# Mamba-2 scan followed by a hardswish MLP: row sums by token through transfers and squares of 32, narrower idle products, decoding steps and the parts of the first weights in another order

## The chip, the cores and the metric

The kernel runs on one core of one Trainium2 chip. The time is the device time in microseconds (us) of one launch; 337.93 us is the median of three runs of the kernel before (337.47 to 337.95). A profile of one more execution goes with it. Engines are named as the profile names them: PE (TensorE, matmuls), PEld (its weight loads, which run beside the matmuls), DVE (VectorE), ACT (ScalarE), POOL (GpSimd) and SP (SyncE, which here only issues transfers; SPq is its queue).

## The reference, cut to what matters

Two blocks follow each other. The first is a state-space scan with batch 4, 8 heads, 768 tokens, head size 32 and state size 16; the second is an MLP over 3072 tokens with 256 inputs, 2048 hidden units and 256 outputs. The MLP weights arrive as 64-bit floating point.

```python
log_a = np.log(np.clip(a, 1e-06, 1.0))
...
cum = np.cumsum(la, axis=-1)                          # within a chunk
L = np.exp(cum[:, :, :, None] - cum[:, :, None, :]) * causal
M = np.einsum('bhin,bhjn->bhij', Cc, Bc) * L
y[:, :, sl] = M @ xc + np.einsum('bhin,bhnd->bhid', Cc, state) * np.exp(cum)[..., None]
state = np.exp(np.sum(la, axis=-1)) * state + (B x, faded to the end of the chunk)
...
h = x @ w_in
g = h * np.clip(h + 3.0, 0.0, 6.0) / 6.0
out = g @ w_out
```

(The einsums are shortened; the results are the same.)

## The kernel before, in words

The 768 tokens are cut into 6 chunks of 128, for all 4 batches and 8 heads at once, so that a chunk has 32 (batch, head) pairs and the MLP sees 512 tokens of it. Each chunk c goes through the scan (decay squares `L`, products of C and B called `cb`, own products with `x` and products with the carried state) and then through the MLP as stage k = c: sixteen tiles f of 128 hidden units, each an accumulation of two fp32 products 128x512 into one of four PSUM banks (`f0` to `f3`), then ACT's `ramp` (L793) and DVE's `times_ramp` (L798), which frees the bank for tile f + 4. The second weight product follows as `first_out` (L811) in stage 0 and in other forms in the later stages. From stage 1 on, the first product is made of three products of rounded parts (hi, lo and less, L754). The scan of chunk k + 1 is written out by hand between the instructions of stage k: every engine has one queue, which it works off in program order, and the kernel says in program order what stands in it.

What the change and the prediction touch:

- **Decoding** (`decode`, L185 to L244). The weights are loaded as raw 32-bit words in eight parts (four of `w_in`, four of `w_out`) and turned into fp32 by steps that `weights(i, n)` advances: ACT copies the top words (L202); DVE masks exponent and sign (L221, L223) and starts the significand (L207); ACT makes the scale in two steps (L227, L229); DVE ends the significand (L211), joins exponent and sign (L234) and multiplies (L244). Three raw buffers are shared by the parts; `load_w(i + 3)` (L144) is issued in the step of L229 and waits until L211 of part i has read its buffer. In stage 0 the list `weave` puts step j of part i behind tile f = 4i - 8 + j; the fifth step of part i stands behind tile f = 4i - 4.
- **Row sums** (`add_up`, L289: a DVE scan). `cum` holds the running sums of log a for 32 rows (pairs) by 768 tokens. Chunks 2 to 5 need them also by token, as a bias for each partition: `turn_cum` transposes four squares 32x128 on PE into PSUM (L336, `c_ps`, bank `f1`), and `by_token` has DVE negate them into `cum_n` (L339). ACT's `decay` (L420) reads `cum_n` as the bias of its exponentials.
- **Rows from DRAM.** `store_rows` (L306, L308) writes `cum` to DRAM, `load_eto` (L328) and `load_decay` (L321) read it back spread over partitions; POOL's `conceal` (L162) masks `L` before ACT's `decay`.
- **Idle products** (`busy`, L528). Two fp32 products 128x512 of the identity with itself, whose result is not used, stand in PE's queue ahead of `scores(0)` (L565), which waits for `cT`, made by DVE (`turn_squares` L500, `part_heads` L510).
- **Parts of w_in** (`in_parts`, L723 on ACT, L726 and L729 on DVE) and of y (`split_y`, L743 on ACT, L744 and L746 on DVE). They live in buffers that earlier tensors leave: the hi part of part 2 in that of `w_in[1]` (tag `w1`), that of part 3 in `w2`, `y_hi` in `w0`.
- **First product of stage 0** (`mlp_in`, L686). Its last 16 products of 32 are cut in halves of 256 columns.

Of the kernel before, what the change touches and what calls it, by code (L numbers as in the profile page):

```python
# [8 lines left out]
FP32 = mybir.dt.float32  # L9
# [3 lines left out]
F32R = mybir.dt.float32r  # L13
# [8 lines left out]
def kernel(  # L22
# [167 lines left out]
    def decode(i):  # L190

        n = NK * FP * P
        top = raws[i].bitcast(U16).rearrange("p (n w) -> p n w", w=4)[:, :, 3]
        lo, hi = (raws[i].rearrange("p (n w) -> p n w", w=2)[:, :, w] for w in range(2))
        s = att.tile([P, n], U16, name="ws")
        e = att.tile([P, n], U16, name="we")
        m = att.tile([P, n], U32, name="wm")  # L200
        for sl in (slice(0, n),) if i != 1 else (slice(0, n // 2), slice(n // 2, n)):
            nc.scalar.copy(out=s[:, sl], in_=top[:, sl])  # L202
            if i == 1 and sl.start == 0:
                yield

        def significand():
            nc.vector.tensor_scalar(  # L207
                out=m, in0=hi, scalar1=0xFFFFF, scalar2=0x100000,
                op0=ALU.bitwise_and, op1=ALU.bitwise_or)
            yield  # L210
            nc.vector.scalar_tensor_tensor(  # L211
                out=m.bitcast(FP32), in0=lo, scalar=2.0 ** -32, in1=m, op0=ALU.mult,
                op1=ALU.add)
            yield

        parts_m = significand()
        if i == 0:
            next(parts_m)
            next(parts_m)
        yield  # L220
        nc.vector.tensor_scalar(  # L221
            out=e, in0=s, scalar1=0x7FF0, scalar2=None, op0=ALU.bitwise_and)
        nc.vector.tensor_scalar(  # L223
            out=s, in0=s, scalar1=0x8000, scalar2=None, op0=ALU.bitwise_and)
        next(parts_m, None)
        yield
        nc.scalar.activation(e.bitcast(BF16), e, AF.Relu, bias=bias_hi, scale=-8.0)  # L227
        yield
        nc.scalar.activation(e, e.bitcast(BF16), AF.Relu, bias=bias_lo, scale=-1.0)  # L229
        next(parts_m, None)  # L230
        if i and i + NRAW < 2 * NP:
            load_w(i + NRAW)
        yield
        nc.vector.tensor_tensor(out=e, in0=e, in1=s, op=ALU.bitwise_or)  # L234
        if i == 0:
            yield
        m, e = m.bitcast(FP32), e.bitcast(BF16)
        if i < NP:
            dst = w_in[i]
            m, e = (t.rearrange("p (k f) -> p k f", k=NK) for t in (m, e))  # L240
        else:
            dst = w_out[:, (i - NP) * FP:(i - NP + 1) * FP, :]
            m, e = (t.rearrange("p (k f) -> p k f", k=FP) for t in (m, e))
        nc.vector.scalar_tensor_tensor(  # L244
            out=dst, in0=m, scalar=2.0 ** -20, in1=e, op0=ALU.mult, op1=ALU.mult)
# [85 lines left out]

    cum_n = const.tile([P, NC, G], FP32, name="cum_n")

    def turn_cum(c_ps):
        for c in range(2, NC):
            nc.tensor.transpose(out=c_ps[:, c], in_=cum_c[:, c], identity=ident[:G, :G])  # L336

    def by_token(c_ps):
        nc.vector.tensor_scalar(  # L339
            out=cum_n[:, 2:], in0=c_ps[:, 2:], scalar1=-1.0, scalar2=None, op0=ALU.mult)  # L340


    yTs, states, mids, bTs, bss, tmps = {}, {}, {}, {}, {}, {}
# [181 lines left out]
    def busy(n, bank):  # L525

        for _ in range(n):
            nc.tensor.matmul(  # L528
                out=bank.rearrange("p (b i) -> p b i", b=NB), lhsT=ident,
                rhs=ident.unsqueeze(1).to_broadcast([P, NB, P]), start=True, stop=True)  # L530

    def from_state(c, a, pairs=range(NQ)):

# [144 lines left out]

    gTs, outs = {}, {}

    def mlp_in(k, f):
        h = ps.tile([P, TB], FP32, name="h", tag=f"f{f % 4}")
        for j in range(NK):
            n = TB // (1 + (f * NK + j >= NF * NK - 16))
            for t in range(0, TB, n):
                nc.tensor.matmul(  # L686
                    out=h[:, t:t + n], lhsT=w_in[f // FP][:, j, f % FP * P:(f % FP + 1) * P],
                    rhs=yTs[k][:, j].rearrange("p b i -> p (b i)")[:, t:t + n],
                    start=(j == 0 and t == 0), stop=True, skip_group_check=True)
        ramp(k, f, h)  # L690
        times_ramp(k, f, h)

    NJ = NF // 2
    EPS = 2.0 ** -12
# [2 lines left out]
    def in_parts(i):  # L702

        n = FP * P  # L710

        def one(pool, tag):
            t = pool.tile([P, NK, n], F32R, name="w_part", tag=tag)
            return [t[:, j] for j in range(NK)]

        def two(tag):
            return [att.tile([P, n], F32R, name="w_part", tag=tag) for _ in range(NK)]

        hi = one(const, f"w{i - 1}" if i > 1 else f"hi{i}")
        lo = one(const, f"lo{i}") if i < 2 else one(att, "wm") if i == 2 else two("ws")  # L720
        less = one(const, f"less{i}") if i < 2 else one(att, "wm") if i == 2 else two("we")
        for j in range(NK):
            nc.scalar.activation(hi[j], w_in[i][:, j], AF.Copy, scale=(1.0 - EPS / 2) * EPS)  # L723
        for j in range(NK):
            yield
            nc.vector.scalar_tensor_tensor(  # L726
                out=lo[j], in0=hi[j].bitcast(FP32), scalar=-1.0 / EPS, in1=w_in[i][:, j],
                op0=ALU.mult, op1=ALU.add)
            nc.vector.tensor_tensor(  # L729
                out=less[j], in0=lo[j].bitcast(FP32), in1=hi[j].bitcast(FP32), op=ALU.subtract)  # L730
        w_parts[i] = (hi, lo, less)
        yield

    def split_y(k):
        hi = const.tile([P, NK, TB], F32R, name="y_hi", tag="w0")
        lo = att.tile([P, NK, TB], F32R, name="y_lo", bufs=1)
        less = att.tile([P, NK, TB], F32R, name="y_less", bufs=1)
        for a in range(2):
            for u in range(2):
                y = yTs[k][:, u, :, HALF[a]] if k == 1 else ys[k][a, u]  # L740
                h, l = (t[:, u].rearrange("p (b i) -> p b i", b=NB)[:, :, HALF[a]]
                        for t in (hi, lo))
                nc.scalar.activation(h, y, AF.Copy, scale=1.0 - EPS / 2)  # L743
                nc.vector.tensor_tensor(out=l, in0=y, in1=h.bitcast(FP32), op=ALU.subtract)  # L744
        for j in range(NK):
            nc.vector.scalar_tensor_tensor(  # L746
                out=less[:, j], in0=lo[:, j].bitcast(FP32), scalar=-1.0 / EPS,
                in1=hi[:, j].bitcast(FP32), op0=ALU.mult, op1=ALU.add)
        y_parts[k] = (hi, lo, less)
# [41 lines left out]
    def ramp(k, f, h):  # L791

        nc.scalar.activation(  # L793
            gTs[k][:, f], h, AF.Relu, bias=half, scale=1.0 / 6.0)
# [85 lines left out]
    def split_quarter(k):  # L880
# [3 lines left out]

        halves = [g_quarter(k, 1, 1)[:, j * NJ // 2:(j + 1) * NJ // 2] for j in range(2)]
        hi, lo, less = quarter_parts[k] = [], [], []
        homes = ((ffn, "wide"), (ffn, "back")), ((const, "w0"), (att, "y_lo"))
        for where, g in zip(homes, halves):
            h, l = (home(*w) for w in where)
            hi.append(h)  # L890
# [213 lines left out]
            sums(c)  # L1104
        mix(c)

    def results(c):
        if c == 1:
            keep(c)
        split_y(c)  # L1110
        if TURN <= c < NC - 1:
            take(c)
        if TURN < c < NC - 1:
            renew(c)
# [69 lines left out]
    for k in range(NC):  # L1184
        gTs[k] = ffn.tile([P, NF, TB], FP32, name="gT")
        c, ahead = k + 1, k + 2
        if k == 0:
            for f in range(NF):
                mlp_in(k, f)
                for i in weave.get(f, []):  # L1190
                    weights(i, 1)
                if f in (6, 8):
                    diff_exp(c, f // 2 - 3)
            weights(NP + 1, 1)
            add_up(ends_at[1])
            store_rows()
            load_eto(c)
            rows(ahead)
# [6 lines left out]
            for i in range(NP):  # L1205
                for b in range(NB):
# [3 lines left out]
                    if (i, b) == (1, 0):  # L1210
                        renew(0)
                    if (i, b) == (1, 1):
                        c_ps = ps.tile([P, NC, G], FP32, name="c_ps", tag="f1")
                        turn_cum(c_ps)
                        by_token(c_ps)
                    if (i, b) == (2, 0):
                        conceal(ahead, 0)
                        conceal(ahead, 1)
# [4 lines left out]
                    elif (i, b) == (1, 3):  # L1223
# [1 line left out]
                        wake(c)  # L1225
                        turn(c, 0)
                        load_bc(ahead)
                        for n in (0, 0, 1):
                            next(ins[n])
                    elif (i, b) == (2, 3):  # L1230
                        decay(ahead, 0)
# [5 lines left out]
                        next(ins[1])  # L1237
                    elif (i, b) == (3, 1):
                        own_products(c)
                        results(c)  # L1240
                        next(ins[2])
                        decay(ahead, 2)
                    elif (i, b) == (3, 2):
                        rows(ahead + 1)
                        decay(ahead, 3)
                        from_start(ahead)
                    elif (i, b) == (3, 3):
                        for q in range(NB):
                            ends(ahead, q)
            lead_on(c)  # L1250
            next(ins[2])
            next(ins[2])
            continue
        if c == NC:
# [129 lines left out]
```

## Time and profile before

| what | value |
|---|---|
| median of 3 runs | 337.93 us (337.47 to 337.95) |
| the profiled execution, its time | 337.99 us |
| its span, first to last instruction | 336.2 us |
| PE busy | 329.7 us (98%) |
| DVE / ACT / POOL busy | 265.4 (79%) / 207.8 (62%) / 130.3 us (39%) |
| stage 0, first product (L686) | 21.4 to 49.0 us |
| stage 0, second product (L811) and scan of chunk 1 | 49.0 to 84.4 us |

How to read it: a group's line gives the code line, engine, operation, output <- inputs, shapes and count, then busy time and mean duration, then the idle time of the engine just before it and what ended that. A timeline line gives the start and the length of a run of equal instructions, and in brackets the idle time before it with its releaser. Consecutive instructions of one engine overlap in these rows, because a row ends when the result is written; so two starts, not two lengths, tell what an instruction costs its queue. An fp32 matmul shows as two records, one for each pass.

### The profile page before, as it was taken

Reading aid. Unit: us, or ns where it says so; the run is one execution under the profiler, and the core shown is the slowest. Engines: PE = TensorE matmul, PEld = TensorE weight load, DVE = VectorE, ACT = ScalarE, POOL = GpSimd, SP = SyncE. Lnnn points to the kernel's source line nnn. Section 1 sums busy time; section 2 is a strip of 40 time slices with the busy share of each in tenths; the row PEclk is TensorE's granted clock in tenths of the full one; section 3 lists DMA queues with packets and bytes.
Section 4 is the critical chain, followed back from the end, with each engine's and each line's share of the span. In section 5 each row is a group of like instructions: output and inputs, shape, how many; then the busy total and the mean of one; then the engine's idle time right before and its main releaser. Section 6 shows DMA issues by size and latency. Waiting matters only on the chain.

```text
span 336.2 us, 8325 instructions
## 1 busy us (share of the span) xinstructions
PE 329.7 (98%) x3361; PEld 272.4 (81%) x3361; DVE 265.4 (79%) x418; ACT 207.8 (62%) x448; POOL 130.3 (39%) x124
## 2 busy tenths in 40 slices
PE   7999999999999999999999999999999999999995
PEld 5464788888778888888888888888888888899994
DVE  6889999977899729969949558938678958599973
ACT  4788887747987571677662577643487221677661
POOL 2200000180744796179983078771058740000000
PEclk9999999999999999999999999999999999999999
DMA  8969960655950215229207258100142001210001
GB/s 174 168 251 225 197 253 19 171 75 140 178 39 1 61 34 116 47 35 108 49 2 162 36 73 76 37 4 10 27 71 20 2 4 17 29 20 0 2 0 62
DMA packets 89605, 25.15 MB, mean 75 GB/s; under 512 B 82208, under 2 KB 85952, under 8 KB 89056
## 3 DMA queue, kind: packets, MB, share of 16 engines
q1 hardware_dynamic: 85184, 23.33, 37.3%
q10 hardware_dynamic: 4384, 1.31, 1.8%
q8 instruction: 26, 0.43, 0.5%
q14 instruction: 11, 0.09, 0.1%
HBM read 21.33 MB, written 3.29 MB: 73 GB/s over the span
## 4 chain that ended last, share of the span: by engine, by line
PE 98%; POOL 0%; issue 0%; DVE 0%; ACT 0%; POOLq 0%
PE h L754 33%; PE wb L1002 9%; PE wc L1002 8%; PE o L811 8%; PE h L686 8%; PE wa L1002 8%; PE o_end L966 6%; PE wb L1010 3%; PE y L660 3%; PE y L538 2%; PE cb L565 2%; PE d L363 1%; PE y L583 1%; PE d L376 1%; PE d L528 1%; PE o_end L984 1%
## 5 line engine op out<-in xcount | busy, mean ns | idle before, releaser
L798 DVE SCALAR_TENSOR_TENSOR gT<-gT,h 128x512 f32<-128x512 f32 x96 | 64.6, 684 | 21.2 <-ACT gT L793 19.6
L793 ACT ACTIVATE gT<-h,half 128x512 f32<-128x512 f32 x96 | 65.4, 683 | 23.4 <-PE h L754 21.0
L774 ACT ACTIVATE h<-h 128x512 f32<-128x512 f32 x66 | 38.3, 585 | 36.6 <-PE h L754 36.5
L754 PE MATMUL h<-y_hi,w_part 128*128 128x512 f32 x160 | 51.1, 405 | 0.0
L754 PE MATMUL h<-y_less,w_part 128*128 128x512 f32 x160 | 50.1, 399 | 0.0
L754 PE MATMUL h<-y_lo,w_part 128*128 128x512 f32 x160 | 49.5, 395 | 0.0
L857 POOL TENSOR_TENSOR s<-gT 128x512 f32<-128x512 f32 x16 | 25.3, 1579 | 51.4 <-DVE gT L798 51.4
L754 PEld LDWEIGHTS h<-y_hi,w_part 128*128 128x128 f32 x160 | 29.9, 188 | 7.3 <-DVE gT L798 0.9
L754 PEld LDWEIGHTS h<-y_lo,w_part 128*128 128x128 f32 x160 | 30.0, 188 | 6.9
L420 ACT ACTIVATE L<-L,cum_n 128x64 f32<-128x64 f32 x128 | 31.7, 337 | 4.5 <-POOL L L162 4.5
L754 PEld LDWEIGHTS h<-y_less,w_part 128*128 128x128 f32 x160 | 29.1, 188 | 6.1 <-DVE h L771 0.3
L811 PE MATMUL o<-w_out,gT 128*128 128x256 f32 x128 | 29.1, 381 | 0.0
L686 PE MATMUL h<-yT,w_in 128*128 128x256 f32 (+1 forms) x96 | 27.8, 451 | 0.0
L438 POOL TENSOR_TENSOR tmp<-state,eto 128x256 f32<-128x256 f32 x5 | 3.4, 680 | 62.7 <-DVE state L593 56.0
L811 PEld LDWEIGHTS o<-w_out,gT 128*128 128x128 f32 x128 | 24.0, 190 | 3.4
L686 PEld LDWEIGHTS h<-yT,w_in 128*128 128x128 f32 x96 | 18.2, 190 | 9.3 <-issue 6.7
L857 POOL TENSOR_TENSOR gT<-gT 128x512 f32<-128x512 f32 x16 | 23.9, 1498 | 0.7
L894 DVE TENSOR_TENSOR q_part<-gT,q_part 128x256 fp32r<-128x256 f32 x24 | 21.5, 926 | 0.0
L431 POOL TENSOR_TENSOR bs<-B,L 128x128 f32<-128x128 f32 x24 | 12.0, 523 | 23.6 <-ACT L L420 15.7
L966 PE MATMUL o_end<-v_pair,g_pair 128*128 128x256 f32 x120 | 21.1, 281 | 0.0
L162 POOL TENSOR_SCALAR_AFFINE_SELECT L<-L 64x1024 f32<-64x1024 f32 (+1 forms) x16 | 20.0, 1255 | 2.0 <-DMA L<-cum_d 1.5
L857 POOL TENSOR_TENSOR s<-s,gT 128x512 f32<-128x512 f32 x16 | 20.5, 1290 | 0.0
(164 smaller groups left out, 636.0 us busy)
## 6 DMA issues: line engine op xcount, KB each, us to landing
raw<-in_moe_w_out_dram SPq DMA_DIRECT2D x4, 1024.0 KB
L<-cum_d SPq DMA_DIRECT2D x8, 512.0 KB
xt<-in_x_dram SPq DMA_DIRECT2D x6, 512.0 KB
raw<-in_moe_w_in_dram SPq DMA_DIRECT2D x3, 1024.0 KB
out_dram<-back SPq DMA_DIRECT2D x128, 16.0 KB
pairs<-in_C_dram SPq DMA_DIRECT2D x40, 32.0 KB
B<-in_B_dram SPq DMA_DIRECT2D x5, 256.0 KB
eto<-cum_e SPq DMA_DIRECT2D x20, 64.0 KB
```

The lines of the kernel that those rows point to most:

```text
L162: nc.gpsimd.affine_select(out=t[rows], in_=t[rows], pattern=pattern, compare_op=ALU.is_ge, fill=-1e5, base=base, channel_multiplier=-1)
L420: nc.scalar.activation(Ls[c][:, b, h], Ls[c][:, b, h], AF.Exp, bias=cum_n[:, c, g:g + 1])
L686: nc.tensor.matmul(out=h[:, t:t + n], lhsT=w_in[f // FP][:, j, f % FP * P:(f % FP + 1) * P], rhs=yTs[k][:, j].rearrange("p b i -> p (b i)" ...
L754: nc.tensor.matmul(out=hs_[k, f], lhsT=w[j][:, f % FP * P:(f % FP + 1) * P], rhs=y[:, j], start=(start and j == 0), stop=True, skip_group_ ...
L774: nc.scalar.activation(h, h, AF.Copy, scale=1.0 / EPS + 1.0)
L793: nc.scalar.activation(gTs[k][:, f], h, AF.Relu, bias=half, scale=1.0 / 6.0)
L798: nc.vector.scalar_tensor_tensor(out=g, in0=g, scalar=1.0, in1=h, op0=ALU.min, op1=ALU.mult)
L811: nc.tensor.matmul(out=o[:, b % 2], lhsT=gTs[0][:, f, b * P:(b + 1) * P], rhs=w_out[:, f], start=(f == 0 and b % 2 == 0), stop=True, skip_ ...
L857: nc.gpsimd.tensor_tensor(out=o, in0=p_, in1=q_, op=op)
L894: nc.vector.tensor_tensor(out=l[:, j], in0=g[:, j], in1=h[:, j].bitcast(FP32), op=ALU.subtract)
L966: nc.tensor.matmul(out=ends_["cross" if n == 2 else "squares"][b], lhsT=g_parts[t][n][:, b * P:(b + 1) * P], rhs=w, start=(t == 0 and b < ...
L1002: nc.tensor.matmul(out=bank[:, slot], lhsT=lhs[:, j], rhs=rhs[:, j], start=(clear and j == 0), stop=True, skip_group_check=True)
```

## The change

1. `turn_cum` goes. Behind the second scan `spread_cum` issues four transfers on SP's queue, ahead of `store_rows`, from `cum` into a new tile `cum_q` of 128 partitions (each takes 32 tokens of every chunk, rows of 128 bytes). `by_token` then has DVE transpose `cum_q` in squares of 32 into `cum_t`, and POOL instead of DVE negates `cum_t` into `cum_n`. Both new tiles live in buffers (`wide`, `back`) that are free at that time.
2. The two idle products have 256 columns instead of 512.
3. In `mlp_in` the last 18 products are cut in halves, not the last 16: tile 7 too.
4. In `decode`, the end of the significand (L211) moves from the step of L229 to the step of L227. In stage 0, for parts 2 to 4, the fifth step (L234, L244) is called between `ramp` and `times_ramp` of tile f = 4i - 4, not behind both.
5. The hi part of part 2 moves to tag `w0`, `y_hi` and a later quarter of `g` to `w1`. The first step of `in_parts(2)` (ACT) moves from behind `results(1)` to the group behind `turn(1)`, and its second step (DVE) from behind `lead_on(1)` to the place between `keep(1)` and `split_y(1)`.

```diff
         nc.scalar.activation(e.bitcast(BF16), e, AF.Relu, bias=bias_hi, scale=-8.0)
+        next(parts_m, None)
         yield
         nc.scalar.activation(e, e.bitcast(BF16), AF.Relu, bias=bias_lo, scale=-1.0)
-        next(parts_m, None)
...
-    def turn_cum(c_ps):
-        for c in range(2, NC):
-            nc.tensor.transpose(out=c_ps[:, c], in_=cum_c[:, c], identity=ident[:G, :G])
-
-    def by_token(c_ps):
-        nc.vector.tensor_scalar(
-            out=cum_n[:, 2:], in0=c_ps[:, 2:], scalar1=-1.0, scalar2=None, op0=ALU.mult)
+    def spread_cum():
+        cum_q = ffn.tile([P, NC - 2, G], FP32, name="cum_q", tag="wide")
+        for q in range(4):
+            nc.sync.dma_start(
+                out=cum_q[q * G:(q + 1) * G], in_=cum_c[:, 2:, q * G:(q + 1) * G])
+        return cum_q
+
+    def by_token(cum_q):
+        cum_t = ffn.tile([P, NC - 2, G], FP32, name="cum_t", tag="back")
+        nc.vector.transpose(
+            out=cum_t.rearrange("p c g -> p (c g)"), in_=cum_q.rearrange("p c t -> p (c t)"))
+        nc.gpsimd.tensor_scalar(
+            out=cum_n[:, 2:], in0=cum_t, scalar1=-1.0, scalar2=None, op0=ALU.mult)
...
             nc.tensor.matmul(
-                out=bank.rearrange("p (b i) -> p b i", b=NB), lhsT=ident,
-                rhs=ident.unsqueeze(1).to_broadcast([P, NB, P]), start=True, stop=True)
+                out=bank[:, :256], lhsT=ident,
+                rhs=ident.unsqueeze(1).to_broadcast([P, 2, P]), start=True, stop=True)
...
-    def mlp_in(k, f):
+    def mlp_in(k, f, between):
...
-            n = TB // (1 + (f * NK + j >= NF * NK - 16))
+            n = TB // (1 + (f * NK + j >= NF * NK - 18))
...
         ramp(k, f, h)
+        between()
         times_ramp(k, f, h)
...
-        hi = one(const, f"w{i - 1}" if i > 1 else f"hi{i}")
+        hi = one(const, {2: "w0", 3: "w2"}.get(i, f"hi{i}"))
...
-        hi = const.tile([P, NK, TB], F32R, name="y_hi", tag="w0")
+        hi = const.tile([P, NK, TB], F32R, name="y_hi", tag="w1")
...
-    def results(c):
+    def results(c, more=None):
         if c == 1:
             keep(c)
+            next(more)
         split_y(c)
...
-                mlp_in(k, f)
+                late = [i for i in weave.get(f, []) if f == 4 * i - 4]
+                mlp_in(k, f, lambda: [weights(i, 1) for i in late])
                 for i in weave.get(f, []):
-                    weights(i, 1)
+                    if i not in late:
+                        weights(i, 1)
...
             add_up(ends_at[1])
+            cum_q = spread_cum()
             store_rows()
...
-                        c_ps = ps.tile([P, NC, G], FP32, name="c_ps", tag="f1")
-                        turn_cum(c_ps)
-                        by_token(c_ps)
+                        by_token(cum_q)
...
-                        for n in (0, 0, 1):
+                        for n in (0, 0, 1, 2):
                             next(ins[n])
...
-                        results(c)
-                        next(ins[2])
+                        results(c, ins[2])
...
             lead_on(c)
             next(ins[2])
-            next(ins[2])
```

## The prediction

> **What bounds the kernel now.** I read the page first: its shares by engine, its slices and the chain that ended last. Then I read the waits, and the timelines of PE, DVE, ACT, POOL and SP around the places that the change touches.
>
> ```profile
> PE 98%; POOL 0%; issue 0%; DVE 0%; ACT 0%; POOLq 0%
> ```
> ```profile
> PE   7999999999999999999999999999999999999995
> ```
>
> The chain that ended last is PE from 2 us on. A busy PE may still be a slow one, so I also compared the starts of its rows with what their columns need. From 21.4 us to the end an fp32 row of 512 columns starts 0.43 us behind the last, one of 256 columns 0.216 us (48 rows of L811 last 10.52 us: (10.52 - 0.38) / 47). PE leaves this rhythm only where the kind of product changes, by 0.1 to 0.2 us. So from 21.4 us on only an edit that shortens PE's own queue, or makes PE wait, moves the end. Ahead of 21.4 us PE does wait; there the edit of the idle products lies.
>
> **Transposes by token (L336).** This is the change's surest term.
>
> ```profile
> 58.30 1.24 PE L811 MATMUL o<-w_out,gT 128*128 128x256 f32 x5
> 59.48 0.43 PE L336 MATMUL c_ps<-ident,rowed 32*128 32x32 f32 x4
> 59.83 1.35 PE L811 MATMUL o<-w_out,gT 128*128 128x256 f32 x5
> ```
>
> The first five L811 rows end their starts at 58.30 + 1.24 - 0.38 = 59.16 us, the next five at 59.83 + 1.35 - 0.38 = 60.80 us. Without the four transposes the fifth start would come at 59.16 + 5 x 0.216 = 60.24 us. They cost PE **0.56 us**: 0.43 us of their own and the change of form to and fro. PE is full on both sides, so all of it is won.
>
> What takes their place is off PE. SP issues four more transfers ahead of `store_rows`; the nearest rows are the stores, 0.34 and 0.43 us (L306, L308), and L328 with up to 0.62 us, so 1.4 to 2.5 us, and I take 2.0 us (0.5 each). SP reaches this place with the scan's end at 55.7 us, and behind the four stand the stores, the loads of `eto` and the two loads of `L`, issued at 60.12 and 60.66 us; the last packet of `L` lands at 66.2 us. POOL's `conceal`, which needs it, starts at 68.70 us: 2.5 us to spare, so even the upper bound is covered. `eto` of chunk 1 lands near 61.5 us and is read by ACT at 64.51 us: covered too. DVE's transpose of 128x128 costs, by its rows for 256 columns (0.445 us) and 512 (0.713 us), 0.31 us along their line, against 0.28 us for the L339 that goes: nothing; the transfers it waits for will have landed by 60 us, and it comes at 65.5 us. Behind it on DVE stands L482 (`csT`), which PE reads at 71.3 us. POOL's new negation has no row of its kind. A memset 128x128 of 0.20 us and a two-input product 128x128 of 0.86 us (L431, beside a busy DVE) bound it; I take 0.41 us, L431 alone. It delays `tmp`, the four L431 and `conceal`, hence ACT:
>
> ```profile
> ACT L L420 <- POOL L L162: 4.5, 1, 4.5
> ```
>
> ACT waits 4.5 us for `conceal` and starts L420 at 71.88 us. Behind it are `adds`, more L420, the copies `yT` and `y_hi`, which PE reads at 82.30 us (L754). Between, ACT is idle 0.24 + 1.09 + 0.24 + 0.68 + 0.16 = 2.4 us, and `y_hi` ends 0.5 us ahead. So 2.9 us, or 2.0 us once PE runs 0.9 us earlier, hide up to 0.86 us of POOL. Cost: nothing.
>
> The Trainium skill (GPSIMD Engine Reference, Specifications) says that GpSimd shares its SBUF interfaces with VectorE and suffers from DVE instructions with two SBUF inputs. L431's rows agree (0.41 us early, 0.86 us at 67.1 to 68.7 us, beside L726 and L729); by this rule the negation would lie nearer to 0.86 us, still covered.
>
> **Narrower idle products (L528).**
>
> ```profile
> 13.62 1.98 PE L528 MATMUL d<-ident 128*128 128x512 f32 x4
> ...
> 14.18 0.88 DVE L510 TENSOR_SCALAR cT<-csT,parity 128x512 f32<-128x512 f32 x2
> ...
> 15.16 0.43 DVE L516 TENSOR_TENSOR csT<-csT,eto 128x256 f32<-128x256 f32 x1
> ...
> 15.54 1.04 PEld L565 LDWEIGHTS cb<-cT,bT 32*64 32x64 f32 x64 [0.76 <-issue]
> 15.54 1.29 PE L565 MATMUL cb<-cT,bT 32*64 32x128 f32 x64
> ```
>
> `cT` is there at 14.18 + 0.88 = 15.06 us, and the DVE instruction released by the same semaphore starts at 15.16 us. PE could start `cb` then too, but its queue still holds the fourth idle row: `cb` starts at 15.54 us, the third of its banks later still. With 256 columns the four rows need 4 x 0.216 instead of 4 x 0.43 us and end near 14.9 us. So `cb` comes **0.38 us** earlier; 0 and 0.47 us are the ends (nothing, if `cb` then waits for something that the idle rows cover; 0.09 us more, the wait of bank `f3` for the last idle row). What follows is one chain from `cb` to the first L686: L614 (DVE would be free at 16.28 us and start at 16.50 us instead of 16.88), the sums L583, ACT's `adds`, L660, `yT`. Every wait in it hangs on PE:
>
> ```profile
> PE y L660 <- ACT adds L599: 0.5, 1, 0.5
> ```
>
> One thing does not move along: the raw words of part 1 land at 18.2 us, and ACT's L202 would want them at 18.17 us, a few hundredths that `yT` has to spare. So I keep 0.38 us.
>
> **Tile 7 in halves.** Two products of 2 x 0.43 us become four of 2 x 0.216 us: nothing on PE, since the weight loads (0.19 us) fit under 0.216 us, as they do for tiles 8 to 15 already. The bounds are 0 and 4 x 0.01 us.
>
> **Order of decoding.** No work is added; DVE's order changes. L211 now stands ahead of `times_ramp` of tiles 3, 7 and 11, L234 and L244 (0.69 + 1.22 us) ahead of that of tiles 4, 8 and 12. What is late next is the bank: tile f + 4 needs `times_ramp(f)`. PE starts tile f at 21.37 + 1.707 f us. `times_ramp(4)` ends at 31.81 us, then at about 33.7 us, and tile 8 starts at 35.0 us: 1.3 us to spare. `times_ramp(8)` ends at 39.31 us, then near 40.7 us (DVE's idle 0.62 us ahead of tile 7 gets filled by L211), tile 12 starts at 41.85 us: 1.1 us to spare. Tiles 3 and 7 keep 2 us. In exchange `w_in[3]`, ready at 41.18 us for tile 12 at 41.85 us, comes about a microsecond earlier; with PE 0.38 us ahead its old 0.67 us would have shrunk to 0.3. Raw buffers come free a tile earlier, so the loads of parts 5 to 7 start earlier. All of it is cover for PE, none a gain; if the 1.1 us were gone, PE would pay whatever lies beyond it, once for each of two tiles.
>
> **Parts of the first weights.** ACT's step of part 2 now reads into `w0`, so it waits for DVE's last read of `w_in[0]` (L726, until 69.3 us); behind it on ACT is L420, which waits for POOL until 71.88 us anyway, and 1.15 us of ACT go from 81.7 us into that hole. `y_hi` now waits for the last read of `w_in[1]` (L726, until 79.13 us) and starts at 80.46 us. DVE's step (0.68 + 0.69 us) ahead of `y_lo` fills an idle 1.06 us and delays `y_lo` by 0.3 us; `y_lo` ends at 82.36 us and PE reads it at 84.06 us. Nothing on PE, and DVE is freer at 86 us. From stage 1 on nothing else changes.
>
> **The sum.** 0.56 + 0.38 = 0.94 us. The profiled execution took 337.99 us (span 336.2 us and 1.8 us around it), 0.06 us above the median of the three runs. So 337.05 us for such an execution, 337.0 us for the median.
>
> **Rivals.** (a) *The idle products hide nothing of use*: `cb` waits for something else, or the chain to 21.4 us regains its time. Only the transposes count: 337.99 - 0.56 = 337.4 us. For it: the trace has no start of `cb` without idle rows ahead. Against: all its other inputs are older (`bT` at 13.34 us). Chance 0.15.
>
> (b) *The clock falls; this one ends slower.* Place: 14.9 to 15.2 us, where PE will stand idle. Two rows of L376 (bf16, 512 columns) take 1.06 us at 7.71 us and 0.60 us at 10.98 us, and three of L371 start 0.43 us apart at 6.43 us: so PE starts at half speed and is raised after some 7 us of work. If the new hole counts as idleness, PE falls back to half speed ahead of stage 0. Price: half of the low stretch; a stretch of 3.4 us costs 1.7 us and gives 338.8 us, one of 7.7 us as at the start costs 3.9 us and gives 340.9 us. It decides from the hole that the clock gate tolerates. Against it: PE is idle 0.46 us ahead of 18.07 us and 0.20 us ahead of 20.08 us now, and L686 runs at full speed from 21.4 us. Chance 0.07. The Trainium skill (TensorE: Matmul & The Clock Gate, The HAM clock gate) says that the clock returns to half after about an idle window of 3.4 us; by that rule a hole of 0.3 us changes nothing, and the two present holes don't contradict it.
>
> (c) *A cover fails*: a `times_ramp`, or `cum_n` and `conceal`, comes more than 1.1 or 2.0 us later than I reckon. Each 0.5 us beyond shows at PE: 337.3 to 338.0 us. Chance 0.08.
>
> (d) *The pause at 20.08 us goes too.* L660's last row ahead of it starts at 19.55 + 0.33 - 0.22 = 19.66 us, the next at 20.08 us: 0.42 us inside one group, put down to no other engine. If it is tied to a moment and not to a place in the program, the shift may take it away: 336.6 us. Chance 0.08.
>
> **How the numbers follow.** The forecast, 337.0 us, has 0.62. Its own range is 336.8 to 337.4 us by the bounds of L528 and the spread of the three runs. The range 336.4 to 337.8 us takes in (a), (d) and most of (c) and leaves out (b). A difference under 0.2%, 0.68 us, is about what a measurement of this kernel can't tell from none; the threshold lies at 337.25 us. The forecast lies 0.25 us below it and may come out above in one case of ten, (d) is faster, (a) and half of (c) are not: faster 0.66, same 0.25, slower 0.09.
>
> **What would show it.** Right: L811 without a hole near 59.5 us; `cb` at 15.15 us or little later, L686 at 21.0 us, and PE's starts 0.94 us earlier from 61 us to the end. Wrong: PE idle ahead of L686's tiles 8 and 12, a wait of L754 for `y_hi` at 81.4 us, rows of L686 more than 0.43 us apart (clock), or `cb` released by another engine. I would be wrong altogether if PE's rhythm from 84 us on turned out not to depend on when it begins.

## The result, and the profile after

| | before | after |
|---|---|---|
| median of 20 runs each, same chip | 337.83 us (337.34 to 338.44) | 336.67 us (336.22 to 337.90) |
| ratio | | 0.9969 (95%: 0.9961 to 0.9977) |
| the profiled execution, its span | 337.99, 336.2 us | 337.30, 335.6 us |

The changed kernel is faster by 0.31% (0.23 to 0.39%), 1.05 us by the ratio; 337.0 us had been forecast, 336.4 to 337.8 us was the range. Lines of after that answer to those of before, first from the page, the chain and PE's slices:

```profile
PE 90%; DVE 4%; DMA 3%; issue 1%; SPq 1%; ACT 1%; DVEq 0%
PE   7989999999999999999999999999999999999995
```

PE bounds the kernel as before. The chain now leaves PE at 15.16 us, because there PE really waits for `cT` (the fence of the idle products below), and runs back over DVE and the transfers that `cT` comes from. It also runs over DVE and ACT from about 150 to 165 us (L897 above all); nothing is lost there, as the last line of the table of segments is the same before and after.

The rows of L814 (L811 before) around 59.5 us, from the timeline of PE:

```profile
54.79 8.58 PE L814 MATMUL o<-w_out,gT 128*128 128x256 f32 x39
```

The hole of the transposes is gone: from start to start the rows are (8.58 - 0.38) / 38 = 0.216 us apart, without a break.

The stretch of the idle products, PE, after:

```profile
13.32 1.13 PE L535 MATMUL d<-ident 128*128 128x256 f32 x4
15.16 1.20 PE L572 MATMUL cb<-cT,bT 32*64 32x128 f32 x64 [0.71 <-DVE cT L517]
...
17.64 0.90 PE L667 MATMUL y<-L,xt 64*32 64x64 f32 x64 [0.46 <-ACT adds L606]
...
19.09 0.33 PE L667 MATMUL y<-L,xt 64*32 64x64 f32 x12
20.44 0.75 PE L667 MATMUL y<-L,xt 64*32 64x64 f32 x52 [1.03 <-issue]
21.12 0.68 PE L545 MATMUL y<-csT,mid 32*64 32x64 f32 x16
21.73 1.55 PE L693 MATMUL h<-yT,w_in 128*128 128x512 f32 x3
```

and the end of the same stretch, before:

```profile
19.55 0.33 PE L660 MATMUL y<-L,xt 64*32 64x64 f32 x12
20.08 0.75 PE L660 MATMUL y<-L,xt 64*32 64x64 f32 x52 [0.20 <-issue]
20.76 0.68 PE L538 MATMUL y<-csT,mid 32*64 32x64 f32 x16
21.37 1.98 PE L686 MATMUL h<-yT,w_in 128*128 128x512 f32 x4
```

`cb` starts 0.38 us earlier in these two executions, to the hundredth as forecast (15.16 for 15.54), and L667 0.43 us. Then the lead is lost: behind the same twelfth product PE pauses 1.24 us from start to start (19.20 to 20.44) where it paused 0.42 us, with no releaser but "issue". L693 starts 0.36 us *later* than before.

The third difference was not forecast. PE's weight loads and DVE's scalings in stage 1, before, from the timelines of PEld and of DVE:

```profile
90.93 0.30 PEld L754 LDWEIGHTS h<-y_hi,w_part 128*128 128x128 f32 x2 [0.46 <-DVE gT L798]
...
96.71 0.30 PEld L754 LDWEIGHTS h<-y_hi,w_part 128*128 128x128 f32 x2 [0.40 <-DVE gT L798]
```
```profile
87.63 1.10 DVE L726 SCALAR_TENSOR_TENSOR w_part<-w_part,w_in 128x512 fp32r<-128x512 f32 x1
88.77 1.51 DVE L729 TENSOR_TENSOR w_part<-w_part 128x512 fp32r<-128x512 f32 x1
90.20 1.87 DVE L798 SCALAR_TENSOR_TENSOR gT<-gT,h 128x512 f32<-128x512 f32 x3
```

and DVE after:

```profile
86.70 0.99 DVE L732 TENSOR_TENSOR w_part<-w_part 128x512 fp32r<-128x512 f32 x1
87.62 0.67 DVE L801 SCALAR_TENSOR_TENSOR gT<-gT,h 128x512 f32<-128x512 f32 x1
```

Before, DVE did both steps of `in_parts(2)` ahead of its first scaling of stage 1, at 90.20 us; a bank was late, and PE's weight loads waited for a scaling twice. After, one of the two steps has been done earlier, the scaling starts at 87.62 us, and PE's weight loads wait for no scaling there.

By segments of PE, profiled executions:

| segment | before | after | difference |
|---|---|---|---|
| start to first L686 / L693 | 21.37 | 21.73 | +0.36 |
| to the first L754 / L757 that reads `y_lo`, just behind the last L811 / L814 (stage 0, holds the transposes) | 62.71 | 62.20 | -0.51 |
| to the first `wc` of L1002 / L1005 (stage 1, holds the two waits) | 30.73 | 30.22 | -0.51 |
| to the end | 221.44 | 221.43 | 0.0 |

The sum, -0.66 us, is the difference of the two executions (-0.69).

### The profile page after: what moved, and what is told of

It reads as the page before. It is cut to its first block, busy times and chain, and to the rows that moved or that the text cites. A ratio compares the mean times of both kernels' runs of the same rounds, so it can differ in the third digit from the quotient of the medians.

```text
span 335.6 us, 8329 instructions
## 1 busy us (share of the span) xinstructions
PE 327.6 (98%) x3361; PEld 272.8 (81%) x3361; DVE 264.2 (79%) x418; ACT 208.2 (62%) x448; POOL 130.3 (39%) x125
## 4 chain that ended last, share of the span: by engine, by line
PE 90%; DVE 4%; DMA 3%; issue 1%; SPq 1%; ACT 1%; DVEq 0%
PE h L757 31%; PE wc L1005 8%; PE wb L1005 8%; PE o L814 8%; PE h L693 8%; PE wa L1005 7%; PE o_end L969 6%; PE wb L1013 3%; PE y L667 3%; PE y L545 2%; DVE q_part L897 2%; DMA raw<-in_moe_w_in_dram 2%; PE cb L572 2%; DVE gT L801 1%; DMA pairs<-in_C_dram 1%
## 5 line engine op out<-in xcount | busy, mean ns | idle before, releaser
L757 PE MATMUL h<-y_hi,w_part 128*128 128x512 f32 x160 | 50.9, 403 | 0.0
L757 PE MATMUL h<-y_less,w_part 128*128 128x512 f32 x160 | 50.1, 399 | 0.0
L757 PE MATMUL h<-y_lo,w_part 128*128 128x512 f32 x160 | 49.5, 395 | 0.0
L757 PEld LDWEIGHTS h<-y_lo,w_part 128*128 128x128 f32 x160 | 30.0, 188 | 6.9
L757 PEld LDWEIGHTS h<-y_hi,w_part 128*128 128x128 f32 x160 | 30.1, 188 | 6.7
L757 PEld LDWEIGHTS h<-y_less,w_part 128*128 128x128 f32 x160 | 29.1, 188 | 6.2 <-DVE h L774 0.3
L427 ACT ACTIVATE L<-L,cum_n 128x64 f32<-128x64 f32 x128 | 31.7, 337 | 1.8 <-POOL L L162 1.8
L814 PE MATMUL o<-w_out,gT 128*128 128x256 f32 x128 | 28.8, 381 | 0.0
L693 PE MATMUL h<-yT,w_in 128*128 128x256 f32 (+1 forms) x100 | 27.8, 440 | 0.0
L814 PEld LDWEIGHTS o<-w_out,gT 128*128 128x128 f32 x128 | 24.1, 190 | 3.4
L693 PEld LDWEIGHTS h<-yT,w_in 128*128 128x128 f32 x100 | 18.9, 190 | 8.6 <-issue 5.7
L897 DVE TENSOR_TENSOR q_part<-gT,q_part 128x256 fp32r<-128x256 f32 x24 | 21.5, 923 | 0.1
L162 POOL TENSOR_SCALAR_AFFINE_SELECT L<-L 64x1024 f32<-64x1024 f32 (+1 forms) x16 | 19.2, 1210 | 3.5 <-DMA L<-cum_d 3.1
```

Of the source, the lines that this page charges most:

```text
L162: nc.gpsimd.affine_select(out=t[rows], in_=t[rows], pattern=pattern, compare_op=ALU.is_ge, fill=-1e5, base=base, channel_multiplier=-1)
L427: nc.scalar.activation(Ls[c][:, b, h], Ls[c][:, b, h], AF.Exp, bias=cum_n[:, c, g:g + 1])
L693: nc.tensor.matmul(out=h[:, t:t + n], lhsT=w_in[f // FP][:, j, f % FP * P:(f % FP + 1) * P], rhs=yTs[k][:, j].rearrange("p b i -> p (b i)" ...
L757: nc.tensor.matmul(out=hs_[k, f], lhsT=w[j][:, f % FP * P:(f % FP + 1) * P], rhs=y[:, j], start=(start and j == 0), stop=True, skip_group_ ...
L814: nc.tensor.matmul(out=o[:, b % 2], lhsT=gTs[0][:, f, b * P:(b + 1) * P], rhs=w_out[:, f], start=(f == 0 and b % 2 == 0), stop=True, skip_ ...
L897: nc.vector.tensor_tensor(out=l[:, j], in0=g[:, j], in1=h[:, j].bitcast(FP32), op=ALU.subtract)
```

## The experiments

**Theory F (instructions)**: PE's instructions come in loads of 16384 bytes (packets of queue q8 in the trace). The load that holds what stands behind the twelfth product lands at a moment of its own, and PE goes on some 1.3 us behind the landing, however early it gets there; an earlier `cb` only lengthens the pause. **Rival P (chain)**: every 0.38 us from `cb` on is kept, and the profiled execution was a bad one. For stage 1: **the two waits** were worth 0.5 us, against my "nothing". The runs came in three groups, on three chips (kernel before: 338.20, 338.07, 338.23 us), so ratios are compared.

### 1. The changed kernel with wide idle products

```diff
-                out=bank[:, :256], lhsT=ident,
-                rhs=ident.unsqueeze(1).to_broadcast([P, 2, P]), start=True, stop=True)
+                out=bank.rearrange("p (b i) -> p b i", b=NB), lhsT=ident,
+                rhs=ident.unsqueeze(1).to_broadcast([P, NB, P]), start=True, stop=True)
```

> The changed kernel with the idle products at 512 columns again. Both theories expect cb about 0.38 us later than in the changed kernel (near 15.54 us). The theory of the chain (every 0.38 us from cb to the first L693 is kept) expects a median 0.38 us above the changed kernel's 336.67 us, near 337.05 us, and L693 0.38 us later than it would start otherwise. The theory of the late instructions (the pause in the 64 products of the mask's line L667 ends about 1.27 us after a 16384-byte load of PE's instructions has landed, whenever PE arrives there) expects the pause shorter by what PE arrives later, the rows after it where they were, and a median within 0.2 us of 336.67 us.

Measured: 0.9966 (0.9954 to 0.9977), where the changed kernel has 0.9969 and, run again (8), 0.9970. P's 0.38 us would have been 0.9980. But `cb` started at 15.12 us here, not at 15.54: the whole stretch ahead of it ran 0.5 us earlier in this execution, so this execution can't show where `cb` would stand. Nor does the time decide: the five runs fall into two groups (336.5 and 336.7, then 337.4 to 337.5 us), their median alone, 337.42 against 338.20 us, gives 0.9977, where P puts it, and only the ratio speaks against P. Run 10 asks the same of the kernel before.

### 2. Only the parts in another order

```diff
-        hi = one(const, f"w{i - 1}" if i > 1 else f"hi{i}")
+        hi = one(const, {2: "w0", 3: "w2"}.get(i, f"hi{i}"))
...
-                        for n in (0, 0, 1):
+                        for n in (0, 0, 1, 2):
...
-                        results(c)
-                        next(ins[2])
+                        results(c, ins[2])
...
             next(ins[2])
-            next(ins[2])
```

> The kernel before with only the parts of the first weights in another order. My prediction counted this part at nothing: median near 337.83 us. The rival, read from the traces: DVE does the step of part 2 before it needs to scale tile 0 of stage 1, the bank of tile 6 comes late, and PE loses about 0.3 us near 90.9 us and 0.27 us near 96.7 us; moving the step takes both waits away. It expects 0.5 to 0.6 us less, near 337.25 us, the first scaling of stage 1 near 88 us instead of 90.2 us, and no wait of the weight load L754 for gT.

Measured: 337.70 against 338.20 us, 0.9986 (0.9977 to 0.9994), -0.50 us. DVE's first scaling starts at 88.14 us, and no weight load L754 waits for `gT`. Stage 1 (first L754 that reads `y_lo` to first `wc`) takes 30.25 us, as after. The rival to my "nothing on PE" holds.

### 3. Half of the raw words of part 1 later

```diff
+        if i == 1:
+            queue.dma_start(out=dst[:, 0], in_=src[:, 0])
+            rest.append((dst[:, 1], src[:, 1]))
+            return
...
+    load_rest()
     busy(2, ps.tile([P, NB * P], FP32, name="d", tag="f3"))
```

(`load_rest` has DVE touch the buffer and SP load the second half.)

> The changed kernel, but the raw words of part 1 come in two transfers of half the size, the second issued only once DVE has reached the idle products, so that fewer packets of 4096 bytes stand ahead of the 16384-byte load of PE's instructions in the DMA engines. If the late load makes the pause in the mask products (L667), the load lands one to two microseconds earlier, the pause shrinks from 1.24 us to 0.4 us or less, L693 starts up to 0.8 us earlier in an execution like the profiled one, and the median lies 0.2 to 0.6 us under 336.67 us with a narrower spread of the runs. If the pause belongs to the place in the program and not to the load, it stays at its 705th PE instruction with the same length, and the median stays at 336.67 us, or is later where the second half comes too late for ACT's L202.

Measured: 341.13 us, 1.0083 (1.0065 to 1.0101): the opposite of the hope. SP issued the second half at 16.25 us, still ahead of the load of instructions, which now started at 19.57 instead of 18.19 us, behind all but the last packets of this half (17.2 to 20.2 us), and landed at 20.52. PE, then the granted clock, from the timeline and the windows:

```profile
19.14 0.33 PE L678 MATMUL y<-L,xt 64*32 64x64 f32 x12
21.86 1.06 PE L678 MATMUL y<-L,xt 64*32 64x64 f32 x52 [2.39 <-issue]
```
```profile
core 0: us, PE busy (x) PEld busy (x) DVE busy (x) ACT busy (x) POOL busy (x), PEclk, DMA share, GB/s
...
20.50:21.00 0.50, 0.00 (x0) 0.00 (x0) 0.00 (x0) 0.00 (x0) 0.00 (x0) 0.97 0.73 213
21.00:21.50 0.50, 0.00 (x0) 0.00 (x0) 0.00 (x0) 0.00 (x0) 0.00 (x0) 0.50 1.00 279
...
27.00:28.00 1.00, 1.00 (x2) 0.34 (x1) 0.97 (x2) 0.28 (x1) 0.00 (x0) 0.60 0.95 266
28.00:28.50 0.50, 0.50 (x2) 0.19 (x1) 0.50 (x1) 0.50 (x2) 0.00 (x0) 1.00 1.05 406
```

(The column ahead of the last two is the granted clock.) PE goes on 1.34 us behind the landing: the load makes the pause, as F says. The pause of 2.61 us brought what my rival (b) had feared at another place: from about 21 to 27.8 us PE had half its clock.

### 4. Only the row sums by transfers

Part 1 of the change (`spread_cum` and `by_token`), put into the kernel before.

> The kernel before with only the row sums changed: the four transposes on PE go, four transfers, a DVE transpose of 32-squares and a negation on POOL come. My prediction: the rhythm of the L811 rows has no hole near 59.5 us, nothing else waits, 0.56 us less, near 337.27 us. The rival: the later loads of L (issued 2.3 us later in the changed kernel) and the negation push conceal and the y_hi that PE reads at 82.3 us, so that less than 0.56 us is left, or nothing: 337.5 to 337.8 us.

Measured: 337.45 against 338.20 us; the ratio, 0.9986 (0.9965 to 1.0007), is blurred by one run of 341.47 us among twelve. The transposes' hole is gone, and stage 0 takes 62.35 us instead of 62.71. But the profiled execution, 338.90 us, lost time in stage 1 (31.59 instead of 30.73 us). PEld, DVE and POOL there:

```profile
97.78 0.30 PEld L761 LDWEIGHTS h<-y_hi,w_part 128*128 128x128 f32 x2 [1.24 <-DVE gT L805]
```
```profile
93.92 1.52 DVE L733 SCALAR_TENSOR_TENSOR w_part<-w_part,w_in 128x512 fp32r<-128x512 f32 x1
```
```profile
91.44 3.46 POOL L162 TENSOR_SCALAR_AFFINE_SELECT L<-L 128x1024 f32<-128x1024 f32 x3 [1.46 <-DMA L<-cum_d]
```

SP comes 2 us later to the next loads of `L` (82.45 for 80.48 us before), POOL's `conceal` waits for them and now lies beside DVE's step L733, which takes 1.52 instead of 0.68 us. Of the 1.24 us, 0.40 us stand in the kernel before too (the fence of stage 1 above), so the rest is what stage 1 lost. The four transfers are not always free: their cover, which I reckoned at 66 to 82 us, has an end at 94 us that I did not look at. In the changed kernel SP comes to those loads at 80.92 us; run 5 shows why.

### 5. The changed kernel with the old order of decoding

The moves of `next(parts_m, None)` and of the fifth step are undone.

> The changed kernel with the steps of decoding in the order of before. My prediction: the order is cover only, so the median stays within 0.1 us of the changed kernel's on the same chip; w_in[3] is ready near 41.2 us instead of 40.0, while PE reaches tile 12 at 41.85 us or some tenths earlier. The rival: with PE ahead of where it was before, this cover is gone and PE waits for w_in[3] or for a scaling at tile 12, up to 0.5 us: median 0.2 to 0.5 us above the changed kernel's.

Measured: 0.9957 (0.9938 to 0.9976), beside 0.9970 (0.9951 to 0.9989) for the changed kernel on that chip. PE has no hole between 21.31 and 46 us. DVE's scan, behind which SP issues the four transfers, in the changed kernel and then here, and a wait of PE's weight loads that is here alone:

```profile
53.74 1.21 DVE L289 TENSOR_TENSOR_SCAN rowed<-rowed 32x512 f32<-32x512 f32 x1
```
```profile
54.45 1.21 DVE L289 TENSOR_TENSOR_SCAN rowed<-rowed 32x512 f32<-32x512 f32 x1
```
```profile
95.66 0.30 PEld L757 LDWEIGHTS h<-y_hi,w_part 128*128 128x128 f32 x2 [0.49 <-DVE gT L801]
```

Counted from the first L693, the scan starts at 32.01 us in the changed kernel and at 33.14 us here (the kernel before has 33.14 too). So the new order of decoding lets SP begin 1.13 us earlier and pays for nearly all of the delay that the four transfers bring here: SP comes to the next loads of `L` 59.2 us behind the first L693 in the changed kernel, 60.6 us here and 59.1 us in the kernel before. In time the order of decoding gains nothing that these runs can tell; whether the old one is 0.35 us better, as the medians have it (336.82 and 337.17 us), lies inside the intervals and stays open.

### 6. Each mask in one product of 512 columns

```diff
-        n = NH // 4
+        n = NH
         for h in range(0, NH, n):
```

> The changed kernel with each mask in one product of 512 columns instead of four of 128, which takes 96 instructions from PE's queue ahead of 6 us and leaves the columns as they are. If only the place in the mask products L667 mattered, the pause stays behind the same product (the 12th of the second half) and the median moves by 0.1 us or less. The theory of the late instructions: PE takes its instructions in loads of 256, so every load is asked for 96 instructions later in the program; now two loads fall into the quick stretch from 15.1 to 21 us. One is asked for near 15.4 us, stands behind the 4096-byte packets of part 1 and is wanted near 17.9 us, in the first half of L667; the next is asked for when PE goes on and wanted in the last L545 products. The old pause is gone, two new ones stand at those places, 1 to 2 us and about 0.5 to 1 us: median 1 to 3 us above the changed kernel's, and more if a pause of over 2 us halves the granted clock as in the third run.

Measured: 345.71 us, 1.0218 (1.0186 to 1.0251). My count was wrong by a factor of two: the masks lose 24 products and their 24 weight loads, 48 instructions, not 96. Records below are PE's matmuls and weight loads in order of time, counted from 0; in the changed kernel the pause stands behind record 698, and 256 instructions earlier lies record 443. With 48 fewer ahead, this kernel's record 443 is what was 491, an own-sum product of L590, and its record 698 is what was 746, in the second half of L667. PE:

```profile
16.23 0.76 PE L590 MATMUL y<-xt,bs 64*32 64x64 f32 x53
19.80 0.45 PE L590 MATMUL y<-xt,bs 64*32 64x64 f32 x11 [2.81 <-issue]
...
22.91 0.87 PE L667 MATMUL y<-L,xt 64*32 64x64 f32 x36
25.82 0.67 PE L667 MATMUL y<-L,xt 64*32 64x64 f32 x28 [2.04 <-issue]
...
27.47 1.22 PE L693 MATMUL h<-yT,w_in 128*128 128x512 f32 x1
```
```profile
17.00:19.00 2.00, 0.00 (x0) 0.00 (x0) 2.00 (x6) 0.00 (x0) 0.00 (x0) 1.00 0.39 154
19.00:21.00 2.00, 0.70 (x32) 0.46 (x39) 0.99 (x1) 0.67 (x3) 0.00 (x0) 0.50 0.49 104
21.00:31.00 10.00, 7.96 (x164) 5.12 (x149) 3.43 (x6) 5.00 (x9) 0.00 (x0) 0.50 0.78 275
```

The pauses stand behind this kernel's own records 443 and 698, the numbers of the table at run 8, though other products stand there: the pause in the second half of L667 has moved from its 12th to its 36th product, 24 products with their 24 weight loads on. The two loads landed at 18.57 and 24.56 us; PE went on 1.23 and 1.26 us later. PE passed record 187, 256 ahead of the first pause, at 11.9 us, but that load started at 17.61 us, behind the packets of `x` (the last at 15.0 us) and as those of part 1 ran out (the last at 18.17 us). L693 is 5.93 us later than in run 8, and the half clock until 32.6 us, (32.6 - 27.5) / 2 = 2.6 us, is the rest of the 8.5 us to that run's median. The kernel has fewer instructions and the same columns, and is slower than before by 7.6 us.

### 7. Half of part 1 behind the load

As 3, but `load_rest` stands behind the first product of `multiply(0)`, and the copy of that half behind all of `yT`.

> The changed kernel with the second half of the raw words of part 1 issued behind DVE's first L621 product (near 17.1 us, so that its packets come after the load of PE's instructions that is asked for near 16.6 us), and ACT's copy of this half put behind all four yT. The theory of the late instructions: the load starts near 17.3 us instead of 18.2 and lands near 18.3, PE goes on 1.3 us later, near 19.6 us; the pause is 0.3 to 0.5 us from start to start instead of 1.24, L693 starts near 20.9 us instead of 21.73, and the median lies 0.2 to 0.6 us under the changed kernel's. What could spoil it: the second half lands after 21.5 us, w_in[1] comes later than tile 4 needs it at 27.8 us, and the gain is lost there again (median as the changed kernel's, or up to 0.5 us above). If the pause has nothing to do with the load, nothing moves ahead of 21.7 us.

Measured: 0.9971 (0.9952 to 0.9989), no gain over the changed kernel (0.9970). SP issued the half at 17.12 us, none of its packets was ahead of the load, and the load still started at 17.82 us, 0.88 us after PE passed record 443 (16.94 us).

```profile
16.75 0.85 PE L601 MATMUL y<-xt,bs 64*32 64x64 f32 x64 [0.42 <-issue]
...
19.46 0.33 PE L680 MATMUL y<-L,xt 64*32 64x64 f32 x12
20.24 0.75 PE L680 MATMUL y<-L,xt 64*32 64x64 f32 x52 [0.45 <-issue]
```

PE itself was 0.5 us late here, by another pause ahead of L601 whose cause stays open: from the last `cb` to the first L601 it took 0.69 us from start to start, 0.39 us in run 8 and 0.20 to 0.25 us in all others. So neither split of part 1 is better than the changed kernel. Even with nothing ahead of it the load took 0.88 us to start, 0.95 to land and 1.47 until PE went on, 3.3 us, and PE took 2.63 us for the 256 instructions that should hide it.

### 8. The changed kernel again

> The changed kernel once more, beside the other three on their chip. Ratio to the kernel before near 0.997. The theory of the late instructions expects that the start of L693 in this execution again lies 1.3 us behind the landing of the 16384-byte load that is asked for near 16.6 us, plus the 1.3 us that PE needs for the rest of the products, and that the time of the execution follows it.

Measured: 0.9970 (0.9951 to 0.9989), L693 at 21.54 us. All kernels but run 6 together, times of their profiled executions (records as in run 6; `load` is the packet of 16384 bytes in queue q8):

| kernel | PE passes record 443 | load starts | lands | PE at record 698 | PE goes on | behind the landing |
|---|---|---|---|---|---|---|
| before | 16.95 | 17.88 | 18.82 | 19.67 | 20.08 | 1.26 |
| after | 16.52 | 18.19 | 19.16 | 19.20 | 20.44 | 1.28 |
| 1 | 16.45 | 17.74 | 18.73 | 19.16 | 20.00 | 1.27 |
| 2 | 16.64 | 17.95 | 18.94 | 19.35 | 20.32 | 1.38 |
| 3 | 16.54 | 19.57 | 20.52 | 19.25 | 21.86 | 1.34 |
| 4 | 17.05 | 17.95 | 19.30 | 19.77 | 20.70 | 1.40 |
| 5 | 16.52 | 17.71 | 18.79 | 19.24 | 20.03 | 1.24 |
| 7 | 16.94 | 17.82 | 18.77 | 19.57 | 20.24 | 1.47 |
| 8 | 16.60 | 17.73 | 18.87 | 19.23 | 20.25 | 1.38 |
| 9 | 17.14 | 18.17 | 19.44 | 19.86 | 20.78 | 1.34 |
| 10 | 16.55 | 17.96 | 19.04 | 19.27 | 20.33 | 1.29 |

The last column holds within 0.23 us while the landing moves by 1.8 us. Passing record 443 near 16.5 us instead of 17.0 us hardly makes the load start earlier: 17.71 to 18.19 us (19.57 in run 3), against 17.82 to 18.17 us. The early ones meet the last packets of part 1, which leave at 18.2 to 18.4 us. That a load is asked for as PE passes the record 256 ahead is inferred from these times; no row shows the request.

### 9. Row sums and parts together, nothing else

> The kernel before with the row sums by transfers and the parts of the first weights in another order, nothing else. If these two carry the whole gain (0.56 us for the transposes, 0.5 us for the two waits at 90.9 and 96.7 us), the median lies 1.0 to 1.1 us under that of the kernel before, the same as the changed kernel's. If the narrower idle products hold the 0.38 us of my prediction, a part of the gain is missing here: 0.7 us under it or less.

Measured: 337.06 against 338.23 us, 0.9968 (0.9956 to 0.9981): the whole gain of the change, without the idle products, tile 7 and the decoding. (Its profiled execution, 337.70 us, was its longest run and has the wait of run 4 in a milder form, 0.69 us; its scan, in the old order of decoding, starts 33.1 us behind the first L693.)

### 10. Only the narrower idle products

> The kernel before with the idle products at 256 columns, nothing else. My prediction: everything from cb on moves by 0.38 us, median 0.38 us under the kernel before. The theory of the late instructions: cb starts up to 0.4 us earlier, the pause in L660 grows by as much, since the load of PE's instructions starts near 17.8 us however early PE asks; L686 starts 1.2 to 1.4 us behind its landing plus the 1.3 us of the remaining products as ever, and the median lies within 0.15 us of the kernel before.

Measured: 338.29 against 338.23 us, 1.0003 (0.9994 to 1.0012). P's 0.9989 lies outside.

```profile
15.23 1.20 PE L565 MATMUL cb<-cT,bT 32*64 32x128 f32 x64 [1.27 <-DVE cT L510]
...
19.15 0.33 PE L660 MATMUL y<-L,xt 64*32 64x64 f32 x12
20.33 0.75 PE L660 MATMUL y<-L,xt 64*32 64x64 f32 x52 [0.84 <-issue]
21.01 0.68 PE L538 MATMUL y<-csT,mid 32*64 32x64 f32 x16
21.62 1.55 PE L686 MATMUL h<-yT,w_in 128*128 128x512 f32 x3
```

`cb` 0.31 us earlier than before, the twelfth product 0.40 us earlier, and nothing left of it behind the pause, which took 1.06 us here instead of 0.42.

## Why the prediction was right, and where it was not

The time came out 0.33 us from the forecast because two errors, of 0.4 and 0.5 us, nearly cancelled. That is luck: of the two terms of the sum one held and one was lost, and a term that I had put at nothing took its place.

- **Transposes, 0.56 us: right.** The hole is gone; stage 0 is 0.51 us shorter in the profile, and runs 2 and 9 leave 0.9986 - 0.9968, about 0.6 us, for them, from runs on two chips whose intervals allow half a microsecond either way.
- **The four transfers: cover right at 66 to 82 us, size and reach not.** SP took 2.72 us, over my upper bound of 2.5 (2.0 forecast); ACT's L427, at 72.18 us instead of 71.88, stayed covered, but the 2.5 us of spare ahead of `conceal` were used up: POOL waited 0.78 us for the second half of `L`. POOL's negation took 0.53 us (0.41 forecast), DVE's transpose 0.30 (0.31). I followed the delay to `L` of the chunk at hand and not to the next one. In stage 1, near 96 us in the changed kernel's time, PE's weight loads wait for a scaling in every other kernel that has the transfers: 1.24 us in run 4, 0.69 in run 9, 0.59, 0.49 and 0.47 in runs 6, 5 and 7, 0.27 and 0.19 in runs 1 and 3. The two executions of the changed kernel have none, and neither has run 2, which has the new order of the parts without the transfers.
- **Idle products: the failed step is "Every wait in it hangs on PE" and with it "So I keep 0.38 us".** The 0.38 us at `cb` were right for an execution like the profiled one, and so was the chain to L667; runs 1 and 2, whose idle products are wide, have `cb` at 15.12 and 15.31 us, waiting for `cT`, so there was less to win in them from the start. The pause at 20.08 us stood in my own text, as rival (d), but I took it for something that could only go or stay. It hangs on the load, not on PE; an early PE waits longer. That is rival (a) in its second form, "the chain to 21.4 us regains its time", which had 0.15. Worth: 0.0 us (run 10).
- **Parts of the first weights: the failed step is "Nothing on PE, and DVE is freer at 86 us. From stage 1 on nothing else changes."** It was worth 0.5 us (run 2). The freer DVE was the point: I had judged PE full from 21.4 us on by the distance of its rows, and the list of waits of the kernel before had, for L754, the sum of the two holes:

```profile
PEld h L754 <- DVE gT L798: 0.9, 2, 0.5
```

  The waits are those of PE's weight loads, 0.46 and 0.40 us. PE's own matmuls start at 90.28, 90.93 and 91.50 us there, where 0.46 us is the rhythm, so the first cost PE 0.30 us; the second, by the same count at 96.71 us, 0.24 us. Together they are a term of 0.54 us.
- **Tile 7 and decoding, 0: right in time** (runs 5 and 9), **but not without effect.** I looked at their cover for the banks alone. The order of decoding gives back 1.13 us of the transfers' delay (run 5). In their profiled executions runs 5 and 9, without it, wait 0.49 and 0.69 us in stage 1, but have a stage 0 of 61.92 and 61.98 us instead of 62.20; what of this is the order's doing stays open.
- **Rival (b), the clock**: at 14.9 to 15.2 us nothing happened, at holes of up to 1.27 us there. The mechanism is real elsewhere: in pauses of 2.61 and 3.02 us (runs 3 and 6) the granted clock fell to half.

The sum with what the runs showed: -0.56 (transposes, still the prediction's term from the rows) -0.50 (parts, run 2) +0.0 (the rest) = -1.06 us, against -1.05 us by the ratio. The agreement to a hundredth is chance, as the intervals of the runs are some tenths wide.

## What to carry to other kernels

Follow a gain to the next thing that comes at a moment of its own, a transfer or a load of instructions; there it ends, and a pause that names no releaser is a likely place. Read the small waits of the bounding engine one by one: here two waits of 0.4 us of PE's weight loads, in a row that I had read past, were half of the gain. A change that only takes instructions away can still move the places where PE's instructions run out: look where they fall, above all among hundreds of small products beside large transfers.

## What the runs showed of the hardware that was not expected

- **Instructions arrive late.** The page has 26 packets in queue q8 of instructions; PE has 6722 matmuls and weight loads, 258 a packet. A pause stood behind PE's record 698 in all kernels, run 6 too. The Trainium skill (Runtime: NRT & Kernel Launch, "Instruction fetch mechanics") says that instructions come in 16 KiB blocks of 256 over a DMA queue of the engine's own while the block before is worked off, and that crossing a block is mostly hidden. The trace agrees with the size; "hidden" does not hold where 256 records of small products and their weight loads take some 2.7 us: PE paused there for 0.42 to 2.61 us from start to start, and for 3.02 us in run 6.
- **The clock falls sooner than after a full idle window.** In run 3 PE's last product ahead of the pause started at 19.25 us, and the clock fell at 20.97 us (0.97 of the slice from 20.5 to 21.0); it was back at 27.8 us (0.60 of 27 to 28), 6.83 us later. The Trainium skill (TensorE: Matmul & The Clock Gate, "Part 1: The HAM clock gate (the "warmup" mystery)") gives a free-running window of 3413 ns; 6.83 us are two of these. It says that the clock falls after at least one idle window of about 3.4 us; here it fell 1.72 us behind the start of PE's last product (20.97 - 19.25), in a hole of 2.61 us, and holes of up to 1.27 us did not bring it down.
